# Moving the weight preparation of one unit, and its loads, to other places of an attention loop written out by hand

## The chip, the cores and the metric

The program runs on one NeuronCore of a Trainium2 chip, in one launch. The metric is device time in microseconds (us) of one execution: 717.48 us before the change, the median of 3 runs from 716.5 to 718.18. The engines have short names in the profile: PE (TensorE, matrix products), PEld (its weight loads), DVE (VectorE), ACT (ScalarE), POOL (GpSimd) and SP (SyncE, which here issues nearly all DMAs).

## The reference

Two batches of eight heads (768 positions, head size 64) go through clustered attention, and the result through two feed-forward blocks:

```python
q_assign = argmax(einsum('bhsd,hcd->bhsc', q_n, c_n), -1)      # 16 centroids a head; k_assign alike
scores = where(q_assign[:, :, :, None] == k_assign[:, :, None, :], 0.125 * q @ k.T, -1e9)
x = (softmax(scores) @ v)                                       # then tokens x 512
h = maximum(maximum(x @ w1, x @ w2), x @ w3);  y = h @ w_out    # 512 -> 768 -> 512
h2 = y @ w_in;  out = maximum(0.01 * h2, h2) @ moe2_w_out       # 512 -> 2048 -> 512
```

All arrays are float32.

## The kernel before, in words

Every large product is made of rounded parts: an operand x is split into a rounded high part and the rest x - high, and high times high, high times rest and rest times high are added up in PSUM. Making the two parts is the work of ACT, DVE and POOL; multiplying is the work of PE.

**Attention.** The heads are taken two at a time: 8 pairs, numbered 0 to 7. A pair has six steps, one for each head and each group of 256 queries; steps are numbered 0 to 47, and r is the step's place in its pair (step 6 is r=0 of pair 1, step 11 its r=5). A step, for one unit of 256 queries, has these operations:

- `S0`, `S1`: the scores of 128 queries, four matmuls each, into one of two PSUM tiles of two banks (L569). A tile is used again when all that reads it has ended.
- `M0`, `M1`: the row maximum on DVE (L575). `X0`, `X1`: the exponentials on ACT (L581), which free the PSUM tile.
- `T0`, `T2`, `T4`: transposes on PE (L618) into one of three PSUM tiles. `E1x`, `E2x`: ACT copies or rounds them (L635). `Bx`: POOL rounds a copy (L639). `Lx`: the rest, on DVE (L647, reads PSUM) or on POOL (L650, reads SBUF), by the table `WAYS`.
- `V0` to `V4`: the product with the values (L663). `Y`, `K1`, `K2`, `SP`, `RA` to `RC`: moving, adding and scaling the result.

Spread over a pair's steps is the preparation of the following pairs: `LD` loads q, k and v of the pair three further on (SP); `QH`, `KH`, `QL` (L375), `KL` (L378 on POOL, in r=1), `VH`, `VL` (L378 on POOL, in r=3) round and split them; `G0`, `G1` are products with the centroids (L421, into the unused end of a score tile), `N0a` to `FB` on DVE and POOL find the nearest centroid, `O0`, `O1`, `P0`, `P1` transpose and scale the one-hot rows. `D0` (r=1) and `D1` (r=3) are the pair's copies, 10 and 6 DMAs on SP (L504) that put the split q and k of the next pair where the scores read them. The first scores that read them are `S0` in r=4 of the pair in work, since scores run two steps ahead.

**What sets the order.** All of it is written out by hand. `ORDER` has six strings, one for each r; `T2/0` means operation T2 of the unit of this step, `S0/-2` that of the unit two steps on, `QL+1` an operation of the next pair. The position of an item in its string (from 0) is its index. Each engine runs its instructions in the order of this list and waits on semaphores for the others. SP is such a queue too: a DMA that waits for a buffer holds all DMAs behind it.

**The first unit of weights.** The weights of the feed-forward blocks lie in units of 2048 columns. Four pieces of 512 columns of the first unit are made inside the attention loop, so that the first products can start right behind it. A piece takes seven calls, `w00` for piece 0 up to `w03` (function `piece`): five calls of one DVE instruction each, of which the second (L159), third (L161) and sixth (L168) work as the first (L157) does, and the fifth is L166 with two inputs; the fourth has one on ACT and one on DVE (L163, L164), the seventh too (L174, L175). `f00` to `f03`, and `f10`, `f11` for the next unit, load a piece's raw words: two DMAs of 512 KB each on SP (L141), into one of two buffers. The table `ONCE` says ahead of which (step, index) each such call stands. At index 20 it stands in r=0 and r=3 among the value products, in r=1 ahead of `D0`, in r=2 between `E12` and `T4`, in r=5 ahead of `L0/0`. At index 29 of r=2 it stands between `S1` and `N0a`; at index 12 of r=1 between `M0` and `T2`; index 2 of r=4 is near its beginning.

**Behind the attention** come the feed-forward blocks, three products for each pair of matrices (L245 to L247), with the later units of weights prepared beside them.

Of the kernel before, what the change touches and what calls it, by code (L numbers as in the profile page):

```python
# [62 lines left out]
)  # L63

ONCE = {
# [8 lines left out]
}  # L74
WAYS = ("DPP", "DDP", "DPA", "DDP", "DDP", "DPA")
ENGINE = {"QH": "A", "QH@1": "P", "KH": "P", "VH": "P", "KL": "P", "KL@0": "D", "VL": "P", "W": "P", "W@1": "D"}
# [936 lines left out]
```

## Time and profile before

| what | value |
|---|---|
| median of 3 runs | 717.48 us (716.5 to 718.18) |
| profiled execution | 716.41 us, span 714.6 us |
| granted TensorE clock | 0.999 of full speed |
| busy: PE, DVE, ACT, POOL | 702.6, 532.0, 379.9, 285.4 us |
| attention, steps 6 to 41 | 48.13 to 228.07 us |
| chain that ended last | PE 86%, DVE 6%, ACT 3% |

The span runs from the first to the last instruction; the time of an execution has a little more around it. Times of rows are us from the span's start. A busy PE is not one at its peak, since a matmul's end is modelled; how long a stretch of the loop lasts is read from where its first matmul and that of the next stretch begin.

### The profile page before, as it was taken

Reading aid. Unit: us, or ns where it says so; the run is one execution under the profiler, and the core shown is the slowest. Engines: PE = TensorE matmul, PEld = TensorE weight load, DVE = VectorE, ACT = ScalarE, POOL = GpSimd, SP = SyncE. Lnnn points to the kernel's source line nnn. Section 1 sums busy time; section 2 is a strip of 40 time slices with the busy share of each in tenths; the row PEclk is TensorE's granted clock in tenths of the full one; section 3 lists DMA queues with packets and bytes.
Section 4 is the critical chain, followed back from the end, with each engine's and each line's share of the span. In section 5 each row is a group of like instructions: output and inputs, shape, how many; then the busy total and the mean of one; then the engine's idle time right before and its main releaser. Section 6 shows DMA issues by size and latency. Waiting matters only on the chain.

```text
span 714.6 us, 10798 instructions
## 1 busy us (share of the span) xinstructions
PE 702.6 (98%) x3878; PEld 602.0 (84%) x3878; DVE 532.0 (74%) x1008; ACT 379.9 (53%) x725; POOL 285.4 (40%) x263
## 2 busy tenths in 40 slices
PE   9999999999899999999999999999999999999997
PEld 6899898898899988888888888888888888888886
DVE  7898989899898778898875499788529945983222
ACT  6888898898799953533222143555433333432220
POOL 3778888797787540111101011223211332221220
PEclk9999999999999999999999999999999999999999
DMA  3886454765540006644444045225505521510112
GB/s 113 208 257 168 113 158 122 192 173 131 147 112 14 1 0 223 220 160 164 164 160 148 6 171 193 103 89 199 184 1 183 182 107 59 187 49 1 45 41 92
DMA packets 29189, 90.00 MB, mean 126 GB/s; under 512 B 4336, under 2 KB 4336, under 8 KB 29136
## 3 DMA queue, kind: packets, MB, share of 16 engines
q1 hardware_dynamic: 28704, 88.13, 38.9%
q10 hardware_dynamic: 432, 1.18, 0.5%
q8 instruction: 31, 0.51, 0.3%
q14 instruction: 22, 0.18, 0.1%
HBM read 68.16 MB, written 3.15 MB: 100 GB/s over the span
## 4 chain that ended last, share of the span: by engine, by line
PE 86%; DVE 6%; ACT 3%; issue 1%; DMA 1%; POOL 1%; SPq 0%; ACTq 0%; DVEq 0%; POOLq 0%
PE h L247 13%; PE h L245 13%; PE h L246 13%; PE y L246 8%; PE y L247 8%; PE y L245 8%; PE s L569 6%; PE o L663 6%; PE t L618 6%; DVE mx L575 2%; PE s L421 2%; PE warm L815 1%; ACT ee L581 1%; DVE el L647 1%; DVE wx L166 1%
## 5 line engine op out<-in xcount | busy, mean ns | idle before, releaser
L279 POOL TENSOR_TENSOR hl<-a,hh 128x512 fp32r<-128x512 f32 x66 | 91.8, 1391 | 344.3 <-ACT hh L278 344.3
L245 PE MATMUL h<-xh,wh 128*128 128x512 f32 x408 | 159.1, 390 | 0.0
L246 PE MATMUL h<-xl,wh 128*128 128x512 f32 x408 | 158.9, 390 | 0.1
L247 PE MATMUL h<-xh,wl 128*128 128x512 f32 x408 | 158.8, 389 | 0.0
L278 ACT CAST hh<-a 128x512 fp32r<-128x512 f32 x66 | 41.1, 622 | 124.7 <-DVE a L272 73.8
L575 DVE TENSOR_REDUCE mx<-s 128x1 f32<-128x768 f32 x96 | 91.3, 952 | 17.2 <-PE s L421 10.3
L245 PE MATMUL y<-hh,wh 128*128 128x512 f32 x264 | 102.7, 389 | 0.0
L246 PE MATMUL y<-hl,wh 128*128 128x512 f32 x264 | 102.7, 389 | 0.0
L247 PE MATMUL y<-hh,wl 128*128 128x512 f32 x264 | 102.7, 389 | 0.0
L650 POOL TENSOR_TENSOR el<-et,eh 128x512 fp32r<-128x512 f32 x72 | 99.3, 1387 | 3.1 <-ACT et L635 0.2
L569 PE MATMUL s<-k,q 128*128 128x512 f32 (+3 forms) x384 | 89.6, 354 | 5.3 <-ACT ee L581 3.2
L581 ACT ACTIVATE ee<-s,mx 128x768 f32<-128x768 f32 x96 | 87.0, 907 | 11.1 <-DVE mx L575 10.2
L246 PEld LDWEIGHTS h<-xl,wh 128*128 128x128 f32 x408 | 76.6, 188 | 16.6 <-DVE xl L236 0.8
L247 PEld LDWEIGHTS h<-xh,wl 128*128 128x128 f32 x408 | 76.6, 188 | 15.8
L245 PEld LDWEIGHTS h<-xh,wh 128*128 128x128 f32 x408 | 76.6, 188 | 15.7
L270 ACT COPY a<-h 128x512 f32<-128x512 f32 x66 | 38.7, 586 | 93.9 <-PE h L247 92.4
L618 PE MATMUL t<-idf,ee 128*128 128x128 f32 x576 | 78.3, 275 | 1.8 <-DVE rs L591 1.4
L274 DVE SCALAR_TENSOR_TENSOR a<-a,h 128x512 f32<-128x512 f32 x48 | 32.9, 685 | 61.7 <-ACT a L270 61.6
L305 DVE TENSOR_TENSOR acc<-y,acc 128x512 f32<-128x512 f32 x72 | 48.6, 686 | 40.5 <-PE y L247 40.5
L663 PE MATMUL o<-eh,vs 128*128 128x256 f32 x288 | 73.3, 288 | 0.0
L663 PE MATMUL o<-el,vs 128*128 128x256 f32 x288 | 71.8, 282 | 0.0
L569 PEld LDWEIGHTS s<-k,q 80*128 80x128 f32 (+1 forms) x384 | 58.6, 190 | 12.7 <-ACT ee L581 4.6
(103 smaller groups left out, 1166.3 us busy)
## 6 DMA issues: line engine op xcount, KB each, us to landing
raw<-in_w SPq DMA_DIRECT2D x56, 512.0 KB, 3.5
low<-in_w SPq DMA_DIRECT2D x56, 511.5 KB, 3.2
q<-qh SPq DMA_DIRECT2D x28, 192.0 KB, 4.7
k<-kh SPq DMA_DIRECT2D x28, 192.0 KB, 4.6
out_T<-acc SPq DMA_DIRECT2D x12, 256.0 KB, 2.0
rq<-in_qT SPq DMA_DIRECT2D x7, 384.0 KB, 3.5
rk<-in_kT SPq DMA_DIRECT2D x7, 384.0 KB, 4.4
rv<-in_v SPq DMA_DIRECT2D x7, 384.0 KB, 5.8
```

The source lines that it names most:

```text
L245: nc.tensor.matmul(ps, ah, bh, start=(k == 0), stop=False)
L246: nc.tensor.matmul(ps, ah, bl, start=False, stop=False)
L247: nc.tensor.matmul(ps, al, bh, start=False, stop=(k == n - 1))
L278: nc.scalar.copy(hh[:, f, :], a)
L279: nc.gpsimd.tensor_tensor(hlo[:, f, :], a, hh[:, f, :].bitcast(F32), op=ALU.subtract)
L305: nc.vector.tensor_tensor(a, ps, a, op=ALU.add)
L569: nc.tensor.matmul(ps[:, lo:hi], a[:, c0 : c0 + P], b[:, lo:hi], start=start, stop=not start)
L575: nc.vector.tensor_reduce(mx, un[n]["s", i], axis=AX.X, op=ALU.max, negate=True)
L581: nc.scalar.activation(e, u.pop(("s", i)), AF.Exp, bias=u.pop(("m", i)), scale=1.0, accum_out=u["sum"][:, i, 0:1],)
L618: nc.tensor.transpose(ps[:, kk, i * P : (i + 1) * P], u["e"][i][:, (k + kk) * P : (k + kk + 1) * P], idf,)
L650: nc.gpsimd.tensor_tensor(lo, et, hi.bitcast(F32), op=ALU.subtract)
L663: nc.tensor.matmul(u["o"], vs[:, t, :], u[e][:, t, :], start=(t == 0 and e == "eh"), stop=(t == NQ - 1 and e == "el"),)
```

## The change

Only the table `ONCE` is changed. The calls are the same, 28 for the weights and 6 for the loads.

```diff
-    (4, 11): "f00", (5, 2): "f01", (6, 20): "w00", (7, 20): "w00", (8, 20): "w00", (9, 20): "w00",
-    (10, 20): "w00", (11, 20): "w00", (12, 20): "w00 f02", (13, 20): "w01", (14, 20): "w01",
-    (15, 20): "w01", (16, 20): "w01", (17, 20): "w01", (18, 20): "w01", (19, 20): "w01 f03",
-    (20, 20): "w02", (21, 20): "w02", (22, 20): "w02", (23, 20): "w02", (24, 20): "w02",
-    (25, 20): "w02", (26, 20): "w02 f10", (27, 20): "w03", (28, 20): "w03", (29, 20): "w03",
-    (30, 20): "w03", (31, 20): "w03", (32, 20): "w03", (33, 20): "w03 f11",
+    (4, 11): "f00", (5, 2): "f01", (7, 12): "w00", (8, 20): "w00", (8, 29): "w00", (9, 20): "w00",
+    (10, 20): "w00", (13, 12): "w00", (14, 20): "w00", (14, 29): "w01", (15, 20): "w01",
+    (16, 2): "f02", (16, 20): "w01", (19, 12): "w01", (20, 20): "w01", (20, 29): "w01",
+    (21, 20): "w01", (22, 20): "w02", (25, 12): "w02", (26, 20): "w02", (26, 29): "w02",
+    (27, 20): "w02", (28, 2): "f03", (28, 20): "w02", (31, 12): "w02", (32, 20): "w03",
+    (32, 29): "w03", (33, 20): "w03", (34, 2): "f10", (34, 20): "w03", (37, 12): "w03",
+    (38, 20): "w03", (38, 29): "w03", (40, 2): "f11",
```

Before, one call stands in each of the steps 6 to 33. After, none stands in r=0 and r=5, one each in r=1, r=3 and r=4, and two in r=2, from step 7 to step 38. The loads `f02`, `f03`, `f10` and `f11` stand at the beginning of r=4, behind the copies `D0` and `D1` of the pair.

## Rows read from the trace of the kernel before

**Rows 1.** Stretches, pairs 1 to 5, feed-forward: length, busy PE PEld DVE ACT POOL, clock, DMA.
```profile
48.13:77.16 29.03, 29.03 (x231) 27.39 (x230) 26.05 (x54) 25.91 (x55) 24.21 (x25) 1.00 0.55 142
77.16:107.60 30.44, 29.57 (x230) 27.43 (x229) 27.90 (x56) 26.79 (x56) 25.03 (x25) 1.00 0.54 142
107.60:138.92 31.32, 29.80 (x230) 27.42 (x229) 28.17 (x56) 26.21 (x55) 25.34 (x25) 1.00 0.66 172
138.92:169.00 30.08, 29.39 (x231) 27.44 (x230) 27.98 (x56) 26.59 (x57) 25.03 (x25) 1.00 0.62 163
169.00:201.66 32.66, 29.95 (x231) 27.45 (x230) 29.28 (x56) 26.87 (x56) 24.70 (x25) 1.00 0.44 116
340.00:715.00 375.00, 370.96 (x1637) 306.95 (x1635) 239.08 (x412) 126.39 (x217) 80.27 (x58) 1.00 0.31 112
```

**Rows 2.** Busy time by stretch: r=0 of pairs 2 to 5 (steps 12, 18, 24, 30), added up.
```profile
sum 23.62, PE 20.35 PEld 17.45 DVE 23.25 ACT 16.83 POOL 15.15; mean PE 5.09 PEld 4.36 DVE 5.81 ACT 4.21 POOL 3.79
```

**Rows 3.** Busy time by stretch: r=0 of pairs 1 and 6 (steps 6, 36), r=4 of pair 1.
```profile
48.13:52.94 4.81, 4.81 (x39) 4.34 (x38) 4.72 (x9) 4.45 (x10) 3.80 (x5) 1.00 0.64 125
201.66:206.46 4.80, 4.80 (x39) 4.33 (x38) 4.71 (x8) 4.45 (x10) 3.79 (x5) 1.00 0.00 0
68.84:72.75 3.91, 3.91 (x32) 3.74 (x31) 3.65 (x10) 3.73 (x8) 2.62 (x4) 1.00 0.01 3
```

**Rows 4.** Timeline around the seam of steps 17 and 18: DVE (start, length, engine, line).
```profile
106.91 1.77 DVE L166 SCALAR_TENSOR_TENSOR wx<-raw,wt 128x512 uint32<-128x512 uint32 x1
...
109.21 0.94 DVE L575 TENSOR_REDUCE mx<-s 128x1 f32<-128x768 f32 x1
```

**Rows 5.** Timeline around the same seam: POOL.
```profile
106.67 3.15 POOL L650 TENSOR_TENSOR el<-et,eh 128x512 fp32r<-128x512 f32 x2
```

**Rows 6.** Timeline of step 18: PE, with its idle time and what ended it.
```profile
111.23 0.50 PE L569 MATMUL s<-k,q 128*128 128x512 f32 x1 [1.01 <-ACT ee L581]
```

**Rows 7.** Busy time by stretch: r=4 of pairs 3 and 5 (steps 22, 34), added up.
```profile
sum 9.39, PE 8.29 PEld 7.48 DVE 7.21 ACT 7.47 POOL 6.82; mean PE 4.15 PEld 3.74 DVE 3.61 ACT 3.74 POOL 3.41
```

**Rows 8.** Timeline of SP in steps 18 to 22: second half of `f03`, last copy of `D1`.
```profile
117.63 0.33 SPq L141 DMA_DIRECT2D low<-in_w  x1
...
130.47 0.59 SPq L504 DMA_DIRECT2D k<-oo  x1
```

**Rows 9.** Timeline of step 22: PE, first scores of the next pair.
```profile
131.78 0.47 PE L569 MATMUL s<-k,q 80*128 80x512 f32 x1 [0.51 <-DMA q<-oo]
```

**Rows 10.** Timeline of step 31: DVE.
```profile
178.10 2.34 DVE L166 SCALAR_TENSOR_TENSOR wx<-raw,wt 128x512 uint32<-128x512 uint32 x1
```

**Rows 11.** Timeline of step 31: POOL.
```profile
178.05 1.84 POOL L378 TENSOR_TENSOR kl<-rk,kh 128x768 fp32r<-128x768 f32 x1
```

**Rows 12.** Timeline of step 32: PE.
```profile
181.19 0.63 PE L618 MATMUL t<-idf,ee 128*128 128x128 f32 x4 [1.38 <-DVE rs L591]
```

**Rows 13.** Timeline of step 37: DVE.
```profile
208.09 0.96 DVE L575 TENSOR_REDUCE mx<-s 128x1 f32<-128x768 f32 x1
```

**Rows 14.** Timeline of step 37: POOL.
```profile
207.86 1.27 POOL L650 TENSOR_TENSOR el<-et,eh 128x512 fp32r<-128x512 f32 x1
209.09 1.85 POOL L378 TENSOR_TENSOR kl<-rk,kh 128x768 fp32r<-128x768 f32 x1
```

**Rows 15.** Timeline of steps 8 and 9 (r=2 and r=3): DVE.
```profile
60.13 0.96 DVE L575 TENSOR_REDUCE mx<-s 128x1 f32<-128x768 f32 x1 [1.58 <-PE s L421]
61.01 0.42 DVE L161 TENSOR_SCALAR wx<-wx 128x512 f32<-128x512 f32 x1
61.34 0.68 DVE L647 TENSOR_TENSOR el<-t,eh 128x512 fp32r<-128x512 f32 x1
62.15 0.36 DVE L432 TENSOR_REDUCE m<-s 128x12 f32<-128x192 f32 x1
...
66.00 0.96 DVE L575 TENSOR_REDUCE mx<-s 128x1 f32<-128x768 f32 x1 [0.60 <-PE s L421]
```

**Rows 16.** Timeline of step 8: POOL.
```profile
61.98 2.53 POOL L650 TENSOR_TENSOR el<-et,eh 128x512 fp32r<-128x512 f32 x2
```

3 rows, old and new, of the table ONCE are left out of this document.

## The prediction, made before the changed kernel was run

> **What bounds the kernel now.** I read the busy time by stretch first, cut where a pair's first transposes begin on PE, then the same for single steps, and then the timelines at the places where a step is too long. In the stretches the reader is to see that the pairs issue the same work on PE in different times: pair 1 takes 29.03 us with PE busy throughout, pairs 2 to 5 take 30.44, 31.32, 30.08 and 32.66 [rows 1]. Together that is 124.50 against 4 x 29.03 = 116.12: 8.38 us in which PE waits for another engine. The feed-forward blocks have PE busy for 370.96 of 375.00 us [rows 1]; they follow the attention on PE, so what the attention gains moves the end by as much. The kernel is bound by PE, and all that the change can win lies in those 8.38 us. PE's granted clock is 1.00 in every one of these stretches [rows 1], so no term for the clock enters.
>
> **The call that leaves r=5.** In step 17 it takes 1.77 us on DVE [rows 4], because POOL's two `el` began 0.24 earlier, at 106.67 [rows 5], and DVE's instruction ends only after the first of them (3.15 / 2 = 1.58, so 108.25). Behind it on DVE are `L0` and the maximum `M1` of step 18, which therefore starts at 109.21 [rows 4]; the exponential on ACT waits for it, the score tile is not free, and PE stands 1.01 us before `S1` [rows 6]. So r=0 is long in pairs 2 to 5: 23.62 for four [rows 2]. Pair 1's r=0 has a call itself but none in the r=5 ahead (the first call is in step 6) and takes 4.81; pair 6's has none in either and takes 4.80 [rows 3]. So the stall belongs to the call in r=5 and not to the one in r=0. Gain: 23.62 - 4 x 4.81 = 4.38. Taking the r=0 call away is worth 0 on PE by the same two rows. Nothing else is late at that seam: with no call in r=5, PE is busy for the whole of both r=0 in rows 3.
>
> **The loads.** SP is a queue. The second DMA of `f03` waits there for the last call of the piece before and goes at 117.63, `D0` and `D1` stand behind it, and the last copy goes at 130.47 [rows 8]; the scores that read the copies are held 0.51 us at 131.78 [rows 9]. The r=4 of pairs 3 and 5, where `f03` and `f11` stood ahead of the copies, take 9.39 together [rows 7], against 3.91 each without [rows 3]: gain 9.39 - 2 x 3.91 = 1.57. In the new places the buffer is given back in steps 14, 21, 31 and 38, ahead of steps 16, 28, 34 and 40. What now queues behind a load is `LD` and the next pair's `D0`. Two DMAs of 512 KB are 1.05 MB, some 7.4 us at the 142 GB/s of pair 1 [rows 1]; the first reader of `LD`'s data is `G0`, three steps on, 3 x 29.03 / 6 = 14.5 us. So the cost is 0, and any delay beyond 7 us would show in full on PE; upper bound 1 us.
>
> **The rest of the lost time** is 8.38 - 4.38 - 1.57 = 2.43. Of this 1.38 is PE's wait before `T0` of step 32 [rows 12], behind the fifth call of `w03` in step 31, which took 2.34 [rows 10]: POOL's `kl` had begun at 178.05, 0.05 ahead of it [rows 11], and held it to 179.89; the work itself then took 0.55. The other 1.05 are short waits in the r=1 and r=2 that follow a late seam; I let them go with it (between 0 and 1.05).
>
> **The calls in r=1** stay, and the fifth call of `w03` moves to step 37. What each of them meets can be read in the r=1 of step 37, behind an r=5 and r=0 without a call, as all will be: `M0` ends at 208.09 + 0.96 = 209.05 [rows 13]. A DVE instruction starts some 0.08 before the one ahead of it ends (60.13 + 0.96 = 61.09, next at 61.01 [rows 15]), so the call starts at 208.97. POOL's `el` runs to 207.86 + 1.27 = 209.13 and `kl` follows from 209.09 [rows 14], 0.12 behind the call. The call waits 0.16 for `el`, works 0.42 (one input, rows 15) or 0.55 (two), and `kl` waits for it. That is 0.6 to 0.7 us on DVE, and DVE has 1.58 idle before the next step's `M0` [rows 15]. Cost 0; upper bound, if `kl` comes first, the 1.38 of rows 12 a step. In steps 19 and 31 an ACT instruction comes ahead of the exponential too; ACT is busy 25.91 of 29.03 and has as many of them as before, so 0.
>
> **The second call in r=2.** It stands behind `L0`, which runs from 61.34 for 0.68 [rows 15], so it starts at 61.94. POOL's pair of `el` starts at 61.98 [rows 16]: DVE is 0.04 ahead. It then costs 0.42 and moves `N0a` from 62.15 to 62.28, by 0.13, and by at most 0.3 more in steps 14 and 20, where the first of the two calls has two inputs. DVE waits 0.60 before the `M0` of r=3 [rows 15], which takes this in: 0. If POOL is first, the call waits for one `el` (2.53 / 2 = 1.27 [rows 16]) to 63.25, `N0a` starts at 63.59, 1.44 late, and 0.84 is left behind the idle 0.60. Over the five steps with `N0a` (8, 14, 20, 26, 32) that is at most 4.2 us. I take 0 since the nearest rows have DVE first, with 0.2 in all for what the five small shifts may leave.
>
> At the two long calls above the engine that started first kept the other waiting: POOL by 0.24 and 0.05, to DVE's cost [rows 4, 5, 10, 11]. The Trainium skill says it as a rule (SBUF — State Buffer, Who interferes with whom): "Whoever issues first gets the shared pair for the whole instruction; the other fully blocks". The trace agrees in those rows; by the rule a lead of 0.04 us is enough in r=2, and were POOL the first there the rule would give rival A.
>
> **Sum.** -4.38 - 1.57 - 2.43 + 0.2 = -8.2 us. The profiled execution took 716.41, so it would take 708.2; the median of the runs stands 1.07 above it, which I leave as it is: 709.3.
>
> **Rivals.**
> A. POOL first at the second call of r=2. For: 0.04 us is little, and POOL's and DVE's starts hang on different chains. Against: both hang on PE's scores and transposes of that step. It adds half to all of 4.2: 711.4 to 713.5.
> B. The seam is not the call's doing but POOL's two `el` themselves. For: they stand ahead of the late `L0`. Against: steps 35 and 36 have them too, and 4.80 [rows 3]. Then only 1.57 + 1.38 come: 714.5.
> C. Slower: `M0` of r=1 ends after `kl` began, so that POOL is first at every call of r=1, and by the lateness at those of r=2 as well. It decides at 0.12 us, the lead in step 37 [rows 13, 14]; step 31 is such a case. Price: 2 x 1.38 for two-input calls (steps 31, 37), 4 x 1.25 for the others (0.55 - 0.42 less), 7.8; and 4.2 in r=2: 717.48 - 8.2 + 12.0 = 721.3. In r=1 alone: 717.1, no change.
> D. The change does not reach the end: PE comes earlier to the feed-forward blocks, but their second unit, loaded later by `f10` and `f11`, is not ready, and the 8 us are waited there: 717.5. For: both loads come 7 and 8 steps later. Against: step 40 is still 8 steps ahead of the end of the attention.
>
> **How the numbers follow.** Forecast 0.68, with a range of its own of 708.2 to 710.7; A 0.13, B 0.05, C in both places 0.05, C in r=1 alone 0.04, D 0.05. A change of under 0.2% (1.4 us) is about what a measurement of this kernel cannot tell from none. Faster by more: the forecast, A and B, 0.86; within it: D and C in r=1 alone, 0.09; slower: 0.05. The range has the forecast with the 0.8 us by which the runs scatter, A, and B at its end: 708.0 to 714.6.
>
> **What would show it.** Right: r=0 of every pair at 4.8, r=4 at 3.9, each pair from 1 to 5 at 29.0 to 29.3; no call of r=1 over 0.9 us, and the second call of r=2 at 0.42 (0.68 in step 38) with the first `el` behind it a little longer. Wrong: calls of 1.4 to 1.7 us in r=2 with the next maximum late (A), of 2 us in r=1 with `T0` of r=2 waiting (C), an r=0 still near 5.8 (B), or waits for `wh` in the first feed-forward products (D).

## The result and the profile after

The changed kernel takes 707.62 us (median of 4 runs, 707.27 to 708.09) against 717.49 for the kernel before beside it (716.5 to 718.18): 9.87 us less, a ratio of 0.9862 with a 95% interval of 0.9848 to 0.9876. The profiled execution took 707.71 us with a span of 705.9. The forecast was 709.3 with a range from 708.0 to 714.6: the direction and every place but one (step 39, below) were as forecast, but the gain was larger by 1.7 us, and the time lies 0.4 below the range.

Busy time by stretch after the change, pairs 1 to 5 and then pair 6 (from and to, length, then PE, PEld, DVE, ACT and POOL busy), to be read beside [rows 1]:

```profile
47.49:76.53 29.04, 29.04 (x231) 27.40 (x229) 26.24 (x54) 25.89 (x55) 24.36 (x25) 1.00 0.63 150
76.53:105.53 29.00, 29.00 (x230) 27.38 (x229) 26.57 (x56) 26.29 (x55) 24.85 (x25) 1.00 0.62 169
105.53:134.53 29.00, 29.00 (x230) 27.37 (x229) 26.68 (x55) 26.68 (x56) 24.84 (x25) 1.00 0.52 130
134.53:163.54 29.01, 29.01 (x230) 27.40 (x229) 26.64 (x55) 26.18 (x55) 24.61 (x25) 1.00 0.61 167
163.54:192.56 29.02, 29.02 (x231) 27.39 (x230) 26.40 (x55) 26.43 (x56) 24.57 (x25) 1.00 0.51 126
192.56:219.36 26.80, 26.68 (x206) 24.85 (x205) 24.95 (x47) 25.27 (x54) 23.08 (x23) 1.00 0.44 111
```

In pairs 1 to 5 the length and PE's busy time are the same to the hundredth: PE waits for nobody. The sums of single steps say it too. First the four r=0 of pairs 2 to 5, which took 23.62 before [rows 2]; then the r=4 of steps 22 and 34, 9.39 before [rows 7]:

```profile
sum 19.23, PE 19.23 PEld 17.35 DVE 18.86 ACT 18.00 POOL 15.50; mean PE 4.81 PEld 4.34 DVE 4.71 ACT 4.50 POOL 3.87
```

```profile
sum 7.82, PE 7.82 PEld 7.49 DVE 7.34 ACT 7.61 POOL 5.26; mean PE 3.91 PEld 3.74 DVE 3.67 ACT 3.81 POOL 2.63
```

The two close meetings went as read. Timeline of step 8 after, DVE and then POOL: the second call (L161) starts at 61.30, 0.04 ahead of POOL's two `el`, and takes 0.42, and it is those that grow from 2.53 [rows 16] to 2.76.

```profile
60.37 0.42 DVE L159 TENSOR_SCALAR wx<-raw 128x512 uint32<-128x512 uint32 x1
60.70 0.68 DVE L647 TENSOR_TENSOR el<-t,eh 128x512 fp32r<-128x512 f32 x1
61.30 0.42 DVE L161 TENSOR_SCALAR wx<-wx 128x512 f32<-128x512 f32 x1
61.63 0.35 DVE L432 TENSOR_REDUCE m<-s 128x12 f32<-128x192 f32 x1
...
61.34 2.76 POOL L650 TENSOR_TENSOR el<-et,eh 128x512 fp32r<-128x512 f32 x2
```

Timeline of step 37 after: the two-input call (L166), 2.34 in step 31 before [rows 10], takes 0.70, and `kl` behind it 2.30 instead of 1.85 [rows 14].

```profile
199.86 0.70 DVE L166 SCALAR_TENSOR_TENSOR wx<-raw,wt 128x512 uint32<-128x512 uint32 x1
...
198.74 1.27 POOL L650 TENSOR_TENSOR el<-et,eh 128x512 fp32r<-128x512 f32 x1
199.97 2.30 POOL L378 TENSOR_TENSOR kl<-rk,kh 128x768 fp32r<-128x768 f32 x1
```

From the two first traces alone, pairs 1 to 5 go from 153.53 to 145.07, 8.46 less, where 8.38 was read; pair 6 goes from 26.41 to 26.80. The profiled times differ by 716.41 - 707.71 = 8.70; 0.64 of this lies ahead of step 6 (its `T0` starts at 48.13 before and at 47.49 after), where the two kernels do the same. From step 42 to the end both take 486.5 us, so nothing is waited for there (rival D). So steps 6 to 41 gained 8.46 - 0.39 = 8.07 in these two traces, and what is to be explained is why the medians differ by 9.87.

### The profile page after: what moved, and what is told of

Same layout as the page of the kernel before. It is cut to its first block, busy times and chain, and to the rows that moved or that the text cites. A ratio compares the mean times of both kernels' runs of the same rounds, so it can differ in the third digit from the quotient of the medians.

```text
span 705.9 us, 10794 instructions
## 1 busy us (share of the span) xinstructions
PE 699.4 (99%) x3876; PEld 601.4 (85%) x3878; DVE 527.0 (75%) x1008; ACT 379.6 (54%) x725; POOL 285.3 (40%) x263
## 4 chain that ended last, share of the span: by engine, by line
PE 97%; ACT 2%; DVE 0%; issue 0%; ACTq 0%
PE h L247 13%; PE h L245 13%; PE h L246 13%; PE o L663 9%; PE s L569 9%; PE t L618 9%; PE y L247 8%; PE y L246 8%; PE y L245 8%; PE s L421 2%; PE warm L815 1%; PE o L672 1%; ACT ee L581 1%; PE scrap L421 1%; PE s L479 1%
## 5 line engine op out<-in xcount | busy, mean ns | idle before, releaser
L618 PEld LDWEIGHTS t<-idf,ee 128*128 128x128 f32 x576 | 65.4, 142 | 2.7 <-DVE el L647 0.6
```

The lines of the kernel that those rows point to most:

```text
L618: nc.tensor.transpose(ps[:, kk, i * P : (i + 1) * P], u["e"][i][:, (k + kk) * P : (k + kk + 1) * P], idf,)
```

## The experiments

Each kernel below differs from one of the two only in the table `ONCE`; line numbers in its rows can be higher by 23 to 27, since its table has more lines. Where a call is put in or taken out, the names of the pieces in the entries between follow, so that each piece keeps its seven calls. Ratios are to the kernel before, run on the same chip in the same job.

**Is a trace of the kernel before like the next one?** The kernel before, twice more.

> The kernel before, unchanged, for a second trace. The prediction carried the 1.07 us by which its median stands above its profiled execution over to the changed kernel, whose median stands 0.09 below its own. Theory 1: the profiled execution of before was one with short stalls; in another one, pairs 2 to 5 together take more than the 124.50 us of the first trace, by up to 1.7 us, and the changed kernel has no such stalls to vary. Theory 2: the pairs take 124.5 again and the difference lies ahead of step 6 (first trace: T0 of step 6 at 48.13) or in the feed-forward blocks (from step 42 to the end 486.5 us).

> The kernel before once more, unchanged, for a third trace. In the second trace r=4 of step 22 and the step behind it took 5.09 and 5.28 us and r=4 of step 34 5.31, where the first had 4.65, 4.38 and 4.74, and the granted clock fell to half for 6.8 us behind the 1.38 us wait of step 32. Theory: the copies of pairs 3 and 5 come late by 1.6 to 3.5 us in all, different in each execution, and this is what the first trace showed too little of; steps 22, 23 and 34 sum to 13.8 to 15.7 here too, all other steps but 32 agree with the first trace within 0.3. Rival: the difference is ahead of step 6 or in the clock alone; then steps 22, 23 and 34 sum to 13.8.

The kernel before scatters much more than the changed one: in the first of these two jobs its runs lay between 715.24 and 721.4, in the second between 715.08 and 720.1. The two new traces took 721.4 and 716.85 us. Steps 22 and 23 together and step 34 in the first, second and third trace of before, then after the change:

```profile
129.89:138.92 9.03, 8.53 (x66) 7.94 (x65) 7.94 (x17) 7.83 (x17) 6.43 (x8) 1.00 0.90 236
192.53:197.27 4.74, 4.15 (x32) 3.74 (x31) 3.56 (x9) 3.74 (x8) 3.46 (x5) 1.00 0.64 148
```

```profile
129.63:140.00 10.37, 8.79 (x66) 7.97 (x65) 8.85 (x17) 7.59 (x16) 6.17 (x8) 1.00 0.83 225
196.95:202.26 5.31, 4.15 (x32) 3.74 (x31) 3.56 (x9) 3.73 (x8) 4.03 (x6) 1.00 0.61 135
```

```profile
129.33:139.70 10.37, 8.78 (x67) 7.96 (x66) 8.32 (x17) 7.60 (x16) 6.17 (x8) 1.00 0.87 223
193.47:197.71 4.24, 4.16 (x33) 3.75 (x31) 3.56 (x9) 3.73 (x8) 2.95 (x5) 1.00 0.74 167
```

```profile
126.24:134.53 8.29, 8.29 (x66) 7.95 (x65) 7.97 (x18) 7.82 (x17) 6.28 (x8) 1.00 0.45 118
184.25:188.16 3.91, 3.91 (x32) 3.74 (x31) 3.65 (x10) 3.89 (x8) 2.64 (x5) 1.00 0.45 101
```

The reader is to see the third column (PE busy) stay behind the length by 0.50, 1.58 and 1.59 in steps 22 and 23: the late copies cost 13.77, 15.68 and 14.61 less 12.20, that is 1.57, 3.48 and 2.41 us. The first trace was the mildest of the three. Steps 6 to 41 as a whole took 179.94, 185.18 and 180.94 us: of the 1.00 by which the third trace is longer than the first, the copies are 0.84, and of the 5.24 of the second they are 1.91. PE's waits in the second name the copies:

```profile
131.95 0.59 PE L569 MATMUL s<-k,q 80*128 80x512 f32 x2 [0.94 <-DMA k<-oo]
...
199.49 0.59 PE L569 MATMUL s<-k,q 80*128 80x512 f32 x2 [1.16 <-DMA k<-oo]
```

Of the other stretches only step 32 moved by more than 0.3: 11.09 in the second trace against 7.96 in the first and third, and there the clock had part (below). The rival, a difference ahead of step 6, doesn't hold up: `T0` of step 6 starts at 48.13, 47.88 and 47.57, latest in the first trace, which was the shortest of the three.

**The loads alone.**

```diff
-(12, 20): "w00 f02", (19, 20): "w01 f03", (26, 20): "w02 f10", (33, 20): "w03 f11"
+(12, 20): "w00", (16, 2): "f02", (19, 20): "w01", (22, 2): "f03",
+(26, 20): "w02", (28, 2): "f10", (33, 20): "w03", (34, 2): "f11"
```

> The 28 calls as before; only the four loads stand elsewhere, f02, f03, f10, f11 at index 2 of steps 16, 22, 28, 34. Theory of the prediction: the r=4 of steps 22 and 34 fall from 4.65 and 4.74 to 3.9, the r=0 of steps 12, 18, 24, 30 stay at 5.8 to 6.1 and step 31's call at 2.3: 1.6 us less than before, about 715.9. Rival: the scores of r=4 are late because the whole pair is late, not for the copies: no change, 717.5.

Measured: 714.21 us (714.01 to 714.67), ratio 0.9948 (0.9930 to 0.9965). In its trace r=4 of steps 22 and 34 is 3.92 and 3.91, the seams stay at 5.76 to 6.08 and step 32 at 7.96: every place as expected. But the time is 3.3 below the median beside the changed kernel (717.49), and 3.8 below the one of its own job (718.0), not 1.6; and the runs lie within 0.7 us. Some runs of the kernel before had a lower mean clock (last section); against the 15 of that job at 0.999 or more, with a median of 717.35, it is 3.1. In the trace SP is no longer held: the last copy of pair 3's `D1` goes 7 us ahead of `T0` of step 22, which is at 128.61, and `f03` behind it. Before, it went 1.0 us behind that `T0` (130.47 [rows 8], `T0` at 129.46).

```profile
121.66 0.59 SPq L531 DMA_DIRECT2D k<-oo  x1
122.29 0.58 SPq L168 DMA_DIRECT2D raw<-in_w  x1
```

**The calls as in the changed kernel, the loads where they were: behind the last call of a piece.**

```diff
-(16, 2): "f02", (28, 2): "f03", (34, 2): "f10", (40, 2): "f11"
+(14, 20): "w00 f02", (21, 20): "w01 f03", (31, 12): "w02 f10", (38, 29): "w03 f11"
```

> The calls stand as in the changed kernel; each load stands right behind the last call of the piece whose buffer it takes, as before: f02 in step 14, f03 in step 21, both ahead of D1 of their pairs, f10 in step 31 ahead of D0, f11 in step 38 ahead of D1. Theory of the prediction: the calls bring 6.8 of the 8.4 us; r=4 of step 22 (f03 ahead of D1) is again held 0.7, that of step 34 (f10 ahead of D0) up to 0.8, that of step 16 not: 709 to 710, against 707.6 for the changed kernel. Rival: with the calls where they are, SP isn't held by a call and the loads may stand there as well: 707.6.

Measured: 710.86 us (710.6 to 711.19), ratio 0.9901 (0.9881 to 0.9920): 3.2 above the changed kernel, at the same steps (22: 5.36, 23: 5.04, 34: 4.79 in its trace, 2.99 over). So the loads weigh 3.1 to 3.3 us from either side, and the calls 714.21 - 707.62 = 6.59 (medians of different jobs, between which the kernel before moved by up to 1.3).

**Is it the place behind the copies, or that SP isn't held?**

```diff
-(16, 2): "f02", (28, 2): "f03", (34, 2): "f10"
+(19, 0): "f02", (25, 0): "f03", (37, 0): "f10"
```

> The changed kernel with f02, f03 and f10 one half pair later: at the beginning of r=1 (steps 19, 25, 37), so ahead of D0 of the next pair and not behind the copies, but with their buffers given back 5, 4 and 6 steps before, so that SP isn't held by them. Theory 1: what cost time was SP held by a wait for a buffer ahead of the copies; no change from the changed kernel, 707.6, r=4 at 3.9 in all pairs. Theory 2: the 1.05 MB themselves delay the copies behind them in the queue: r=4 of steps 22, 28 and 40 held by 0.5 or more each, 709 to 710.

Measured: 707.57 us (707.26 to 708.17), ratio 0.9865 (0.9844 to 0.9886), as the changed kernel; r=4 is 3.91 or 3.92 in steps 16 to 40. Ahead of the copies the loads do no harm if their buffers are long free. The cost before was SP waiting for a buffer, and the copies starting behind that load.

**The calls of r=5 alone.** They go to index 29 of r=2; r=0 and the loads stay.

```diff
-(11, 20): "w00", (17, 20): "w01", (23, 20): "w02", (29, 20): "w03", (33, 20): "w03 f11"
+(8, 29): "w00", (14, 29): "w01", (20, 29): "w02", (26, 29): "w03", (32, 29): "w03", (33, 20): "f11"
```

> Only the calls of r=5 (steps 11, 17, 23, 29) are moved, to index 29 of r=2 (steps 8, 14, 20, 26); the last call then falls in step 32. Calls in r=0 and the places of the loads stay. Theory of the prediction: r=0 of pairs 2 to 5 at 4.8 (4.4 us less), the short waits behind it gone (1.0 less); step 31 still has the fifth call of w03 with two inputs, but behind a timely seam POOL's kl is no longer ahead: about 0.7 instead of 2.34, so 1.4 less as well. The loads still hold r=4 in pairs 3 and 5 (1.6 stays). 6.8 us less: 710.7, or down to 709.5 if what varies between executions of before lies at the seam. Rival: the call with two inputs in r=1 is long by its kind: 2.3 us again, 1.4 stays, 712. Rival: POOL's two el hold the seam, not the call: 716.

Measured: 709.77 us (709.07 to 710.46), ratio 0.9882 (0.9861 to 0.9904). The seam is confirmed: r=0 of pairs 2 to 5 takes 4.80 to 4.81. The sentence on step 31 is not: its call takes 2.36 again and step 32 is 7.79. That the loads hold r=4 in both pairs was half right: step 22 takes 5.59, but step 34 3.91, where the last call of `w03` stands a step earlier. Timeline of step 31 there, DVE (`K1`, then the call) and then POOL, `kl` 0.03 ahead of the call:

```profile
171.12 0.43 DVE L712 TENSOR_TENSOR acc<-o,tmp 64x256 f32<-64x256 f32 x1 [0.37 <-ACT tmp L706]
...
172.97 2.36 DVE L190 SCALAR_TENSOR_TENSOR wx<-raw,wt 128x512 uint32<-128x512 uint32 x1
...
172.94 1.84 POOL L402 TENSOR_TENSOR kl<-rk,kh 128x768 fp32r<-128x768 f32 x1
```

So a late seam isn't what makes that call long. In its r=0 stood a call with an ACT part, the fourth of a piece, and `K1` in step 31 waited 0.37 for `Y` on ACT. Not every ACT part does this: in step 13 of the same trace, behind a seventh call in r=0, `K1` shows no wait and the call (one input) starts 0.27 ahead of `kl`:

```profile
83.56 0.59 DVE L181 TENSOR_SCALAR low<-low 128x512 uint32<-128x512 uint32 x1
...
83.83 2.03 POOL L402 TENSOR_TENSOR kl<-rk,kh 128x768 fp32r<-128x768 f32 x1
```

**That ACT part out of r=0.**

```diff
-(30, 20): "w03"
+(28, 24): "w03"
```

> As e_seam (calls of r=5 moved to r=2, loads as before), but the fourth call of w03, which has an instruction on ACT, stands in r=4 of step 28 and not in r=0 of step 30. In e_seam the fifth call, in r=1 of step 31, took 2.36 though the seam ahead was timely. Theory: the ACT part in r=0 holds Y on ACT, so K1, K2 and M0 on DVE end 0.35 late while POOL is on time, and kl comes in first; without it the call takes about 0.7, step 32 6.4 instead of 7.8: 1.4 less than e_seam, about 708.4. Rival: a call with two inputs in step 31 is long whatever stands in r=0: 2.36 again, 709.8.

Measured: 708.51 us (707.71 to 710.02), ratio 0.9882 (0.9862 to 0.9902), 1.26 below e_seam, with step 32 at 6.41 instead of 7.79. `K1` no longer shows a wait, and the call starts 0.24 ahead of `kl` (the fourth call's DVE instruction was moved too; that its ACT one counts is read from `K1`'s wait in e_seam):

```profile
172.34 0.83 DVE L190 SCALAR_TENSOR_TENSOR wx<-raw,wt 128x512 uint32<-128x512 uint32 x1
...
172.58 2.31 POOL L402 TENSOR_TENSOR kl<-rk,kh 128x768 fp32r<-128x768 f32 x1
```

**The same cause in another place.** The changed kernel's loads, with calls kept in r=0 and none doubled in r=2:

```diff
-(8, 29): "w00", (14, 29): "w01", (20, 29): "w01", (26, 29): "w02", (32, 29): "w03", (38, 29): "w03"
+(6, 20): "w00", (12, 20): "w00", (18, 20): "w01", (24, 20): "w02", (30, 20): "w02", (36, 20): "w03"
```

> Loads as in the changed kernel; one call in each of r=0 to r=4, none in r=5 and none twice in r=2, from step 6 to step 38: the r=0 calls are kept. The prediction priced a call in r=0 at nothing. By what the long call of step 31 showed there is one exception: a call with an ACT part in r=0 followed by a two-input call in r=1. Here that pair stands in steps 18 and 19 (fourth and fifth call of w01); step 19's call takes 2.3 and step 20 is 1.4 longer; all other pairs 29.0. So 707.6 + 1.4 - 0.4 (step 39, whose 0.4 came from two calls in step 38) = 708.6. Rival: a call in r=0 costs nothing at all: 707.2. Rival: the long call needs a late seam or late copies as well: 707.2.

Measured: 709.03 us (708.74 to 709.67), ratio 0.9891 (0.9873 to 0.9909). Step 19's call takes 2.35, `kl` 0.05 ahead; step 20 takes 7.79, 1.38 over; the other steps of pairs 1 to 5 are at their floor. The step that was picked from the order beforehand is the one that got long. Step 39, expected back at 4.58, is 5.14: a single call in step 38 is enough, which here starts 0.28 behind POOL's `el` and takes 1.55.

```profile
112.87 2.35 DVE L193 SCALAR_TENSOR_TENSOR wx<-raw,wt 128x512 uint32<-128x512 uint32 x1
...
112.82 1.85 POOL L405 TENSOR_TENSOR kl<-rk,kh 128x768 fp32r<-128x768 f32 x1
```

**What the lead of 0.04 us in r=2 is worth.** The second call of r=2 one place later, behind `N0a`:

```diff
-(8, 29): "w00", (14, 29): "w01", (20, 29): "w01", (26, 29): "w02", (32, 29): "w03", (38, 29): "w03"
+(8, 30): "w00", (14, 30): "w01", (20, 30): "w01", (26, 30): "w02", (32, 30): "w03", (38, 30): "w03"
```

> The changed kernel with the second call of r=2 one place later, behind N0a instead of ahead of it. The call then starts some 0.4 us behind POOL's first el instead of 0.04 ahead. Prediction's rival A as a kernel: the call waits for that el and takes 1.2 instead of 0.42 us in steps 8, 14, 20, 26 and 32, N0b, the row sums and M1 of r=3 come 0.8 later; DVE's idle 0.6 before M0 of r=3 takes most of it in: 0 to 0.4 a step, 707.6 to 709.6. If DVE's lateness there were on the path in full, 4 us: 711.6.

Measured: 713.66 us (713.42 to 714.1), ratio 0.9952 (0.9937 to 0.9967): 6.0 above the changed kernel, more than the case "on the path in full". Timeline of steps 8 and 9, DVE and then POOL:

```profile
61.47 1.13 DVE L188 TENSOR_SCALAR wx<-wx 128x512 f32<-128x512 f32 x1
...
64.31 1.48 DVE L191 TENSOR_SCALAR wt<-wx 128x512 uint32<-128x512 uint32 x1
65.71 0.68 DVE L674 TENSOR_TENSOR el<-t,eh 128x512 fp32r<-128x512 f32 x1
66.31 0.94 DVE L602 TENSOR_REDUCE mx<-s 128x1 f32<-128x768 f32 x1
...
61.03 2.71 POOL L677 TENSOR_TENSOR el<-et,eh 128x512 fp32r<-128x512 f32 x2
63.70 1.81 POOL L405 TENSOR_TENSOR vs<-rv,vs 128x768 fp32r<-128x768 f32 x1
```

The first late call makes the next one late: the call of r=3 now comes 0.61 behind `vs` and waits for that too (1.48 against 0.42 of work). The idle before `M0` of r=3 is used up, and r=3 to r=5 of pair 1 take 6.08, 4.50 and 4.68 instead of 5.86, 3.91 and 4.42. Pairs 1 to 5 lose 1.06 to 1.39 each, 6.2 together.

**The changed kernel again, and a version past it.** The second takes the two calls out of step 38 and puts two into r=0:

```diff
-(38, 20): "w03", (38, 29): "w03"
+(6, 20): "w00", (12, 20): "w00"
```

> The changed kernel, unchanged, for a second trace and its scatter beside the kernel before. Theory: what varied between executions of before is gone with the loads and the long calls, so the runs lie within 1 us of each other, at 707.3 to 708.2, pairs 1 to 5 at 29.0 each again, step 39 at 4.97. Rival: the changed kernel was caught in a good moment; then single steps of 0.5 us and more over the first trace turn up, and the runs scatter by several us as those of before do.

> The changed kernel with the two calls of step 38 taken away and two put into the r=0 of steps 6 and 12, so that the preparation ends in step 37. Theory: step 39 falls from 4.97 to 4.58 and nothing else changes, 0.4 us less than the changed kernel, 707.2; two calls in r=0 are free. Rival: the call with an ACT part in step 12 makes the call of step 13 long (it has one input, so 1.8 to 2.1 us): 708.3.

The changed kernel: 707.67 us (707.29 to 708.32), ratio 0.9871 (0.9851 to 0.9891), each pair's length within 0.02 of the first trace. The other: 707.13 us (706.97 to 708.49), ratio 0.9867 (0.9846 to 0.9888). Its step 39 falls from 4.97 to 4.62, but step 17 rises from 4.38 to 4.53; 0.5 us between the medians is within what cannot be told from no change, so it isn't shown to be faster.

## Why the prediction was right, and where it was wrong

- **The seam, 4.38 with 1.05 of short waits behind it.** Right in size and cause: 23.62 became 19.23, and e_seam gave it alone.
- **The call of step 31, 1.38.** Right in size. That the loser is whoever starts second was right too; what puts `kl` first was left open in the text and my first guess in the experiments, a late seam, fell. Shown by e_seam, e_stt and e_r0keep: the fourth call of a piece in r=0, with its ACT instruction (L163), and the fifth behind it in r=1. The two inputs alone do not do it (0.70 in step 37 after), and neither does the seventh call's ACT instruction (L174) in r=0 (step 13 of e_seam). Whether a one-input call would be long behind the fourth isn't shown, since the fifth always follows it. Those three terms, less the 0.2, made 6.6; the medians of e_loads and the changed kernel differ by 6.59.
- **The calls in r=1 and the second in r=2 at no cost.** Right for pairs 1 to 5: `N0a` moved by 0.12 (0.13 read), calls of r=1 took 0.44 to 0.71 on DVE. By the Trainium skill (SBUF — State Buffer, Who interferes with whom) the first to issue keeps the pair of ports that DVE and POOL share. The traces agree: a lead of 0.04 us was enough in both traces of the changed kernel, and e_behind shows the other order. Missed: in step 38, which has no `G0`, the first call starts 0.54 behind POOL's `el` and takes 1.03, and step 39 loses 0.39; 0.2 had been set aside.
- **The loads, 1.57, and the 1.07 left as it was: the step that failed.** The place and the cause were right (SP held, copies late, r=4), the size was not: it measures 3.1 to 3.3 in medians. The step reads "gain 9.39 - 2 x 3.91 = 1.57" and then "the median of the runs stands 1.07 above it, which I leave as it is". Both came from one execution, in which the copies were least late of three (1.57, 3.48, 2.41). Against that one execution the sum was right, 8.2 for the 8.07 found in steps 6 to 41. But the 1.07 was not a constant of the measurement: the changed kernel's median stands 0.09 below its profiled time, so the change takes it away with the rest. Part of it is the same wait in other executions (0.84 of 1.00 in the third trace); how much isn't shown. With the 3.24 of e_calls in place of 1.57 the sum is 6.6 + 3.2 = 9.8, against 9.87. (The 3.28 of e_loads proves nothing here: with the 6.59 it gives 9.87 whatever the cause.)
- **The rivals.** A was priced at most 4.2 and is worth 6.0 as a kernel, since the late call meets the next POOL instruction too. B, C and D did not come; of C's mechanism the price of 1.38 for a two-input call was met in e_r0keep (1.38).

Open: why the copies behind a held SP land so differently from one execution to the next. They are issued within 0.5 us of the same moment, but the first copy of pair 3's `D1` took 4.2, 5.3 and 5.7 us from issue to landing in the three traces of before, and 3.7 in e_loads. Open too is what part the two other things that varied have in the 1.07: the clock (last section), and the time ahead of the first step, which went the other way (`T0` of step 6 lay between 46.95 and 48.13 in all traces here, and the 48.13 is that of the first trace).

## What to carry to other kernels

A wait that ends on a DMA can differ between executions, as here by more than a factor of two; price it from several executions, and where a kernel's runs lie above its profiled one, ask which wait the difference belongs to before carrying it over. Where two engines meet within some tenths of a microsecond, lay their start times side by side and move work so that the short instruction comes first: here a lead of 0.04 us was enough, and giving it up cost 6.0. A load that waits for a buffer belongs behind the short copies of its queue or so late that the buffer is long free; here either did.

## What the runs showed of the hardware that was not expected

In the second trace of the kernel before, the granted TensorE clock fell to the lower of its two levels (1.2 GHz) behind step 32's wait. Stretches around it: 3.40 us with 1.38 of waiting on PE, then 6.80 at the low clock, then full again.

```profile
181.00:184.40 3.40, 2.02 (x16) 1.88 (x16) 3.24 (x7) 1.91 (x5) 2.83 (x4) 0.97 0.92 250
184.50:191.30 6.80, 6.80 (x33) 6.61 (x33) 3.49 (x7) 2.90 (x8) 3.91 (x4) 0.52 0.01 4
191.40:197.00 5.60, 5.60 (x48) 5.42 (x47) 4.74 (x13) 5.05 (x11) 2.60 (x4) 1.00 0.55 143
```

Step 32 took 11.09 instead of 7.96, so it cost 3.1 us. The same 1.38 wait stands in the first and third trace with the clock at 1.00, so the wait alone does not bring it; in the changed kernel, which has no such wait, neither trace shows it.

It is not rare. Of the 59 later runs of the kernel before, 16 had a mean granted clock of 0.998 or less, with a median of 719.0 us; the other 43 have 716.9. The six runs of e_loads, which keeps the wait of step 32 and has no late copies, are all at 1.000, and of all runs with a changed table one, of the version past the changed kernel, is at 0.998 (708.49 us). What brings the fall is not shown.
